# Convolution, GELU and two matmuls: four more blocks in Strassen's form, with more of its sums made by DMA and ScalarE

## The chip, the cores and the metric

The kernel runs on one core of a Trainium2 chip. A core has five engines that run their own instruction lists and wait for each other through semaphores: TensorE (matmul, PE in the profile; PEld is its weight load), VectorE (DVE), ScalarE (ACT), GpSimd (POOL) and SyncE (SP). Sixteen DMA engines move data; transfers are issued from SP, ACT or POOL. On-chip memory is SBUF, and matmuls write to PSUM. The metric is the device time of one launch in microseconds (us).

## The reference

An input `x` of 8 x 4096 tokens with 192 channels is convolved along the tokens, causally, with 7 taps. The taps are a softmax over a weight of 8 heads x 7, and 24 neighbouring channels share a head. The 32768 tokens then go through two matmuls with an exact GELU between them.

```python
w = softmax(weight)                            # 8 heads x 7 taps
x_pad = zeros(B, 6, D) ++ x                    # along the tokens
conv = einsum('hk,bskhg->bshg', w, unfold(x_pad))
h = conv.reshape(32768, 192) @ w_in            # 192 x 2048
g = 0.5 * h * (1.0 + erf(h * inv_sqrt2))
out = g @ w_out                                # 2048 x 192
```

## The kernel before

The tokens are split in two halves of 16384, which lie on partitions 0 to 63 and 64 to 127 and are worked side by side. Each half is cut into 35 blocks (`NB`, L37): six of 256 tokens, then 29 of 512. The 192 channels lie as three groups of 64.

For one block the work goes like this. SP loads `x` as float32 into `xin` (three buffers, `load`, L539; it waits until VectorE has transposed the block three before). VectorE transposes it 32 x 32 into `xT` (`trans`, L706). GpSimd copies six columns of the block before in front of it (`halo`, L639). The seven taps are a multiplication and six multiply-adds on VectorE, each in two pieces of 1024 and 512 columns (`conv`, L731); the last writes `xc` in bf16. For the blocks in `K0` (L73), ScalarE makes the first tap, in three pieces (`first_tap`, L867), at the GELU slots given by `TAPS` of the block two before. TensorE multiplies `xc` by `w_in` (`mm1`, L962) in 16 slices into two PSUM buffers `hp`, and ScalarE turns each slice into bf16 by one GELU into `gT` (L904).

While TensorE makes block n's first product it also makes the second product of block n-1 (`mm2_t`, L1054), interleaved slice by slice. A tile of 64 x 64 of the array is used per matmul, so four matmuls of 512 columns run at once; call four such a round. An ordinary block takes 48 rounds for the first product and 48 for the second. The output, transposed, collects in PSUM banks of `ob`, VectorE transposes it into `osb` (`evac_t`, L363, three per block), and SP stores it (`store`, L551).

Some blocks (`ST`, L72) make the second product in Strassen's form (`mm2_s`, L1101): seven products P1 to P7 in place of eight for two of the three channel groups, plus the ordinary D and E products for the third. That is 44 rounds. It needs sums of halves of `gT` beforehand and sums of the products behind:

- Beforehand: S1 and S3 in four quarters each, Dn and S4 in two halves each (`PART`, L445), written to `sst`. VectorE makes S1, Dn, S4 and the last quarter of S3 (`st_add`, L460). The first three quarters of S3 are two transfers each on GpSimd's queue, a copy and an accumulating one (`st_dma`, L448). Dn needs S1 and S4 needs Dn. The products use them in the order in `TILES` (L378): P5 takes S1, P7 takes S3, P3 takes S4 and P6 takes Dn.
- Behind: six copies on ScalarE (`st_copy`, L484) of P1, P5 and P6 out of PSUM and within SBUF, at slots `AT_COPY`; five sums on VectorE (`st_post`, L503); and three transpositions into `osb` (`st_evac`, L528). TensorE may begin P4 only when the first of these sums (p0) has read its bank, and the next block's second product only when the third (p2) has and P6 is copied.

Every engine works through its list in order. VectorE's order comes from two lists that are merged: `plan` (L764), the taps and input transpositions block by block, and `side` (L796), which says before which step of which block's taps each of the other calls stands (`AT_ST`, `at_ev`). GpSimd's list goes block by block: a halo, then the six transfers of a Strassen block. SP's list goes block by block: the load of three blocks ahead, then a store, which waits for the transpositions.

Of the kernel before, what the change touches and what calls it, by code (L numbers as in the profile page):

```python
# [11 lines left out]
def bass_lightweight_conv__then__act_gelu_exact_kernel(  # L12
# [59 lines left out]
    ST = [m for m in range(M0 + 3, M1) if m % 3 == 0]  # L72
    K0 = {n: i for i, n in enumerate([4, 5, 6, *(n for n in range(9, NB) if n - 3 not in ST)])}  # L73
# [48 lines left out]
    with es:  # L122
# [66 lines left out]
        S_CP = [sem("S_CP%d" % q) for q in range(3)]  # L189
        S_AD = [sem("S_AD%d" % q) for q in range(3)]  # L190
# [116 lines left out]
        def wait_banks(t, m, g):  # L307

            k = G0[m] + g
            if m < M0:  # L310
                if k >= 2:
                    t.wait_ge(S_EVA, k - 1)
            elif g % 2:
                t.wait_ge(S_GELU, SL0[NB] - 1 + g // 2)
            elif M1 - 1 in ST:
                i = ST.index(M1 - 1)
                t.wait_ge(*((S_AC, 6 * i + 4) if g == 0 else (S_EV, EVC[M1] - 2)))
                t.wait_ge(S_DP, 5 * i + 3 + g)
            else:
                t.wait_ge(S_EV, EVC[M1] - 2 + g)  # L320
# [125 lines left out]
        ND = 3  # L446

        def st_dma(e, m, q, h):  # L448

            i, n = ST.index(m), NF // 2 // PART["S3"]  # L450
            dst = ap(sst[1], q * n * TB, [[NF // 2 * TB, 128], [TB, n], [1, TB]])
            src = ap(gT[m % 2], (4 * q * n + h) * TB, [[NF * 2 * TB, 128], [4 * TB, n], [1, TB]])
            if h == 0:
                e.wait_ge(S_GELU, SL0[m] + 2 * (q + 1) * n - 1)
                e.dma_start(dst, src).then_inc(S_CP[q], 16)  # L455
            else:
                e.wait_ge(S_CP[q], 16 * (i + 1))
                e.dma_start(dst, src, accum_op=ALU.add).then_inc(S_AD[q], 16)  # L458

        def st_add(v, m, name, q):  # L460

            g, n = gT[m % 2], NF // 2 // PART[name]

            def a(h, par):
                return ap(g, (2 * q * n + par) * 2 * TB + h * TB, [[NF * 2 * TB, 128], [4 * TB, n], [1, TB]])

            def t(k):
                return ap(sst[k], q * n * TB, [[NF // 2 * TB, 128], [TB, n], [1, TB]])

            i = ST.index(m)  # L470
            v.wait_ge(S_GELU, SL0[m] + 2 * (q + 1) * n)
            if name == "S1":
                ins = v.tensor_tensor(t(0), a(1, 0), a(1, 1), ALU.add)  # L473
            elif name == "S3":
                ins = v.tensor_tensor(t(1), a(0, 0), a(1, 0), ALU.add)
            elif name == "Dn":
                v.wait_ge(S_SA[0], PART["S1"] * i + (q + 1) * n * PART["S1"] // (NF // 2))
                ins = v.tensor_tensor(t(2), a(0, 0), t(0), ALU.add)
            else:
                v.wait_ge(S_SA[2], PART["Dn"] * i + q + 1)  # L480
                ins = v.tensor_tensor(t(3), a(0, 1), t(2), ALU.add)
            ins.then_inc(S_SA[NS.index(name)])

        def st_copy(a, m, k):  # L484

            def xb(r, w=TB):
                return bank(BK[m]["X"], r, w)

            if k > 3:
                a.wait_ge(S_AC, 6 * ST.index(m) + 4)  # L490
            if k in (0, 1, 3):
                st_done(a, m, ("P1", "P5", "", "P6")[k])
            dst, src = (
                (gsm[LO, :], xb(LO)),
                (p5s[UP, :], xb(UP)),
                (p5s[LO, 0 : TB // 2], xb(UP, TB // 2)),
                (uu[LO, :], xb(LO)),
                (uu[UP, :], uu[LO, :]),
                (gsm[UP, :], uu[LO, :]),
            )[k]  # L500
            a.activation(out=dst, in_=src, func=AF.Copy, scale=-1.0 if k > 3 else 1.0).then_inc(S_AC)

        def st_post(v, m, k):  # L503
# [3 lines left out]
            if k == 0:  # L507
                st_done(v, m, "P7")
                v.wait_ge(S_AC, 6 * i + 2)
                ins = v.tensor_tensor(tq[UP, :], bank(BK[m]["Y"], UP), p5s[UP, :], ALU.subtract)  # L510
            elif k == 1:
                st_done(v, m, "P3L")
                v.wait_ge(S_AC, 6 * i + 3)
# [4 lines left out]
            elif k == 3:  # L518
                v.wait_ge(S_AC, 6 * i + 5)
                v.wait_ge(S_DP, 5 * i + 3)  # L520
                ins = v.tensor_tensor(tq[:, :], tq[:, :], uu[:, :], ALU.add)
            else:
                v.wait_ge(S_MM2, MMC[m + 1])
                v.wait_ge(S_AC, 6 * i + 6)
# [3 lines left out]
        def st_evac(v, m, j):  # L528
            i = ST.index(m)
            if j == 2:  # L530
                st_done(v, m, "DE")
                v.wait_ge(S_OUT[m % 2], OUTS[m - 2])
                src = bank(BK[m]["D"])
            else:
                v.wait_ge(S_DP, 5 * i + 5 - j)
                src = (gsm, tq)[j][:, :]
# [14 lines left out]
        def store(e, m):  # L551
# [28 lines left out]
        TAPS = (7, 10, 12)  # L580
        AT_ST = {
            "S1": [(1, 9, 0), (2, 0, 0), (2, 1, 0), (2, 5, -1)],
            "S3": [(2, 5, 1)],
            "Dn": [(2, 0, 2), (2, 5, 2)],
            "S4": [(2, 0, 4), (2, 6, 0)],
            "post": [(2, 11, 0), (3, 0, 0), (3, 2, 0), (3, 6, 0), (3, 9, 0)],
            "ev": [(3, 10, 0), (3, 7, 0), (3, 4, 0)],
        }

        def at_ev(n):  # L590

            if n - 1 in ST:
                return [(2, 15, 0), (3, 4, 0), (3, 4, 0)]
            return [(2, 13, 0) if n == M0 else (3, 0, 3), (3, 5, 0), (3, 5, 0)]

        AT_COPY = {0: (1, 6), 1: (1, 8), 2: (1, 10), 3: (1, 13), 4: (2, 1), 5: (2, 4)}

        @block.gpsimd
        def _(g):
# [72 lines left out]
            for n in range(3, M1 + 2):  # L672
                if n < NB:
                    halo(n)
                if n - 2 in ST:
                    for q, h in ((0, 0), (1, 0), (0, 1), (2, 0), (1, 1), (2, 1)):
                        st_dma(g, n - 2, q, h)

        @block.vector
        def _(v):  # L680
# [83 lines left out]
            plan = []  # L764
            for n in range(2, NB):
                ops = [] if n in K0 else [("t", n, 0)]
                ops += [("c", n, k, q) for k in range(int(n in K0), KS) for q in range(2)]
                if n + 1 in K0:
                    ops[6 if n < 6 else 2 : 6 if n < 6 else 2] = [("t", n + 1, 0)]
                plan.append(ops)  # L770

            def run(op):
                if op[0] == "t":
                    trans(*op[1:])
                else:
                    conv(*op[1:])

# [18 lines left out]
            side = [((M0 + 2, 4 * g, 0), evac, v, M0 - 1, g) for g in range(NG[M0 - 1])]  # L796
            side += [((M0 + 1, 2 * k + 1, 0), weights, v, k) for k in range(6)]
            for n in range(M0, M1):
                todo = []
                if n not in ST:  # L800
                    todo = [(at, evac_t, n, j) for j, at in enumerate(at_ev(n))]
                else:
                    for name, ats in AT_ST.items():
                        for q, at in enumerate(ats):
                            if name == "post":
                                todo.append((at, st_post, n, q))
                            elif name == "ev":
                                todo.append((at, st_evac, n, q))
                            else:
                                todo.append((at, st_add, n, name, q if name != "S3" else ND))  # L810
                side += [((n + at[0], *at[1:]), op, v, *rest) for at, op, *rest in todo]
            for n in range(M1, NB):
                for g in range(NG[n]):
                    side.append(((n + 3, g, 0), evac_half, v, g, 0))
            side.sort(key=lambda q: q[0])
            for b in range(2, NB):
                for o, op in enumerate(plan[b - 2]):
                    while side and side[0][0][:2] <= (b, o):
                        side[0][1](*side[0][2:])
                        side.pop(0)  # L820
                    run(op)
            for q in side:
                q[1](*q[2:])

        @block.scalar
        def _(a):
# [35 lines left out]
            for n in K0:  # L862
                at = taps.get(n, TAPS)
# [54 lines left out]
        def _(t):  # L918
# [135 lines left out]
            def mm2_t(m, ps, i):  # L1054

                w = WS[m]
                if i == 0:
                    if m - 1 in ST:
                        s = ST.index(m - 1)
                        if ps == 0:  # L1060
                            t.wait_ge(S_AC, 6 * s + 4)
                            t.wait_ge(S_DP, 5 * s + 3)
# [38 lines left out]
            def mm2_s(m, e):  # L1101
# [9 lines left out]
                if u == "P6":  # L1111
                    need(S_AC, 6 * i + 1)
                if u == "P4":
                    need(S_DP, 5 * i + 1)
# [5 lines left out]
                else:  # L1120
                    q = NS.index(src)
                    part = k * PART[src] // (NF // 2)
                    if src == "S3" and part < ND:
                        need(S_AD[part], 16 * (i + 1))
                    elif src == "S3":
                        need(S_SA[q], i + 1)
                    else:
                        need(S_SA[q], PART[src] * i + part + 1)
# [80 lines left out]
        def _(sp):  # L1209
# [6 lines left out]
            load(sp, 3)  # L1216
            for n in range(1, NB):
                if n + 3 < NB:
                    load(sp, n + 3)
# [33 lines left out]
```

## Time and profile before

| | |
|---|---|
| median of three runs | 671.5 us (671.0 to 671.69) |
| the profiled execution | 670.93 us |
| its span, first to last instruction | 669.2 us |
| TensorE busy, granted clock | 665.8 us (99%), 1.000 |
| VectorE busy | 604.7 us (90%) |
| ScalarE busy | 587.8 us (88%) |
| GpSimd busy | 91.9 us (14%) |
| packets of hardware / software DMA queues | 49.37 MB, 33.0% / 16.13 MB, 12.1% of the 16 engines' span |
| transfers into `sst` on POOL's queue | 54 of 256 KB |

The busy time is the time in which an engine had at least one instruction at work. The rows of neighbouring instructions on VectorE and ScalarE overlap a little, so the time from start to start is what counts. TensorE's matmul ends are modelled: one row of 376 ns does not mean that a round takes that long. What limits the kernel is read from the chain of work that ended last and from who waits for whom.

### The profile page before, as it was taken

How to read it: one execution, taken by the hardware profiler on the slowest of the kernel's cores; microseconds unless marked ns; L12 is line 12 of the kernel's file. 1: busy time of each engine (PE TensorE's matmuls, PEld its weight loads, DVE VectorE, ACT ScalarE, POOL GpSimd, SP SyncE). 2: the span in 40 equal slices, each digit the busy share in tenths (PEclk: the TensorE clock that was granted, in tenths of full speed). 3: DMA queues.
4: the chain of work that ended last, by engine and by line, in shares of the span. 5: the costliest groups of instructions: out<-in, count | busy, mean ns of one | idle time of the engine just before them, and what ended most of it. 6: DMA issues, size and time to landing. Idle time of an engine off the chain costs nothing.

```text
span 669.2 us, 27224 instructions
## 1 busy us (share of the span) xinstructions
PE 665.8 (99%) x12504; PEld 416.2 (62%) x12504; DVE 604.7 (90%) x703; ACT 587.8 (88%) x659; POOL 91.9 (14%) x115
## 2 busy tenths in 40 slices
PE   9999999999999999999999999999999999999998
PEld 8999655556555655655565556556555655565567
DVE  5989999899999999999999999999999999999633
ACT  8999988899988988898999889888989998898783
POOL 8020000030012003001300120030013001200300
PEclk9999999999999999999999999999999999999999
DMA  9535234273466047515634660485157346602423
GB/s 153 123 86 132 61 72 97 73 132 85 96 143 139 9 96 176 112 36 126 140 84 97 140 143 7 96 176 111 39 127 140 82 97 142 139 8 61 119 63 96
DMA packets 142786, 67.82 MB, mean 101 GB/s; under 512 B 127248, under 2 KB 140880, under 8 KB 142672
## 3 DMA queue, kind: packets, MB, share of 16 engines
q1 hardware_dynamic: 129136, 49.37, 33.0%
q0 software_dynamic: 12416, 16.13, 12.1%
q8 instruction: 98, 1.61, 1.0%
q10 hardware_dynamic: 1120, 0.59, 0.3%
q14 instruction: 16, 0.13, 0.1%
HBM read 28.31 MB, written 25.17 MB: 80 GB/s over the span
## 4 chain that ended last, share of the span: by engine, by line
PE 99%; ACT 0%; DVE 0%; DMA 0%; issue 0%; ACTq 0%
PE hp L999 49%; PE ob L1077 29%; PE ob L1143 13%; PE ob L1039 5%; PE ob L1199 1%; PE hp L1199 1%; PE ob L941 0%; DMA wsb<-in_weight_dram 0%; PE ob L999 0%; ACT dg L846 0%; DVE wcol L701 0%; ACT xc L237 0%; DVE wnm L692 0%; ACT osb L344 0%; ACT wex L833 0%
## 5 line engine op out<-in xcount | busy, mean ns | idle before, releaser
L904 ACT ACTIVATE gT<-hp 128x1024 bf16<-128x1024 f32 x510 | 518.2, 1023 | 68.3 <-PE hp L999 60.5
L999 PE MATMUL hp<-xc,win 64*64 64x512 bf16 (+2 forms) x6036 | 416.8, 366 | 0.1
L757 DVE SCALAR_TENSOR_TENSOR acc<-xT,wcol,acc 128x1024 f32<-128x1024 f32 (+1 forms) x330 | 299.6, 957 | 7.3 <-ACT acc L872 7.3
L999 PEld LDWEIGHTS hp<-xc,win 64*64 64x64 bf16 (+1 forms) x6036 | 190.6, 106 | 126.5 <-ACT xc L237 0.3
L1077 PE MATMUL ob<-gT,wout 64*64 64x512 bf16 x3648 | 248.6, 376 | 0.0
L1077 PEld LDWEIGHTS ob<-gT,wout 64*64 64x64 bf16 x3648 | 116.9, 118 | 83.3
L1143 PE MATMUL ob<-gT,wout 64*64 64x512 bf16 x864 | 109.3, 376 | 0.0
L1143 PE MATMUL ob<-sst,wst 64*64 64x512 bf16 x432 | 88.9, 376 | 0.0
L729 DVE STREAM_TRANSPOSE xT<-xin 128x1536 f32<-128x1536 f32 (+2 forms) x39 | 74.6, 1922 | 9.7 <-DMA xin<-in_x_dram 9.3
L652 POOL COPY xT<-xT 128x18 f32<-128x18 f32 x30 | 28.9, 964 | 330.9 <-DVE xc L757 171.3
L1143 PEld LDWEIGHTS ob<-gT,wout 64*64 64x64 bf16 x864 | 48.8, 118 | 25.2
L757 DVE SCALAR_TENSOR_TENSOR xc<-xT,wcol,acc 128x1024 bf16<-128x1024 f32 (+1 forms) x66 | 61.9, 960 | 0.3
L370 DVE STREAM_TRANSPOSE osb<-ob 128x512 f32<-128x512 f32 x57 | 47.6, 874 | 4.0 <-PE ob L1077 3.7
L455 POOL DMA_DIRECT2D sst<-gT x27 | 19.8, 733 | 175.1 <-ACT gT L904 175.1
L872 ACT ACTIVATE acc<-xT,wcol 128x512 f32<-128x512 f32 (+1 forms) x63 | 43.6, 693 | 0.0
L1039 PE MATMUL ob<-wout,gT 64*128 64x192 bf16 x768 | 41.0, 243 | 0.0
L1143 PEld LDWEIGHTS ob<-sst,wst 64*64 64x64 bf16 x432 | 36.2, 107 | 6.0
L1143 PE MATMUL ob<-gT,wst 64*64 64x512 bf16 x144 | 39.7, 376 | 0.0
L1039 PEld LDWEIGHTS ob<-wout,gT 64*128 64x128 bf16 x768 | 33.4, 94 | 4.8
L458 POOL DMA_DIRECT2D sst<-gT x27 | 33.1, 1227 | 8.0 <-DMA sst<-gT 7.9
L473 DVE TENSOR_TENSOR sst<-gT 128x1024 bf16<-128x1024 bf16 x36 | 24.9, 691 | 10.0 <-ACT gT L904 9.9
L1143 PE MATMUL ob<-sst,wout 64*64 64x256 bf16 x288 | 30.8, 269 | 0.0
(75 smaller groups left out, 268.2 us busy)
## 6 DMA issues: line engine op xcount, KB each, us to landing
out_dram<-osb SPq DMA_DIRECT2D x124, 192.0 KB, 3.4
xin<-in_x_dram SPq DMA_DIRECT2D x116, 192.0 KB, 4.2
sst<-gT POOLq DMA_DIRECT2D x54, 256.0 KB, 4.1
xin<-in_x_dram SPq DMA_DIRECT2D x18, 96.0 KB, 2.4
wout<-in_moe_w_out_dram POOLq DMA_DIRECT2D x4, 192.0 KB, 4.5
win<-in_moe_w_in_dram POOLq DMA_DIRECT2D x4, 96.0 KB, 4.1
win<-in_moe_w_in_dram POOLq DMA_DIRECT2D x2, 192.0 KB, 4.1
xin<-in_x_dram POOLq DMA_DIRECT2D x4, 96.0 KB, 3.9
```

Source lines behind the costliest of these rows:

```text
L370: v.transpose(osb_t(m, j), bank(BK[m][j])).then_inc(S_EV)
L458: e.dma_start(dst, src, accum_op=ALU.add).then_inc(S_AD[q], 16)
L473: ins = v.tensor_tensor(t(0), a(1, 0), a(1, 1), ALU.add)
L652: g.tensor_copy(dst, src).then_inc(S_HALO)
L729: v.transpose(out, src).then_inc(S_TR)
L757: ins = v.scalar_tensor_tensor(dst, src, wk, a, op0=ALU.mult, op1=ALU.add)
L872: a.activation(out=acc[n % 2][:, p * TB : p * TB + w], in_=ap(xT[n % 2], p * XW + HX, [[NP * XW, 128], [1, w]]), func=AF.Copy, scale=wcol[ ...
L904: a.activation(out=ap(gT[n % 2], i * c * 2 * w, dst), in_=ap(ob, 2 * TB, [[4 * TB, 128], *src[1:]]) if u < SL0[1] and u % 3 == 2 else ap(h ...
L999: ins = t.matmul(hbuf(u, slice(fo, fo + fw), o, w), ap(win, f1, [[NP * F, 64], [2, fw]]), xc[n % 2][r, p * TB : p * TB + w], start=(p == 0 ...
L1039: ins = t.matmul(bb[sub], gT[m % 2][r, c0 : c0 + 128], wout[r, CH[sub][i] * C : (CH[sub][i] + 1) * C], start=(ph == 0 and k == 0), stop=(p ...
L1077: ins = t.matmul(bank(BK[m][j], slice(64 * h, 64 * h + 64), w), ap(wout, 64 * hf * NF * C + CH[h][i] * C + j, [[NF * C, 64], [NP, 64]],), ...
L1143: ins = t.matmul(bank(BK[m][bk], slice(64 * cg, 64 * cg + 64), w), wt_, a[r, c0 : c0 + w], start=(e == mine[0]), stop=(e in (mine[-1], GRO ...
```

## The change

- `ST` becomes every second block from 8 to 32: 13 blocks, before 9 (9, 12, ... 33).
- `K0` now has all blocks from 9 on, so ScalarE makes the first tap for all of them. `TAPS` depends on whether the block three before is a Strassen block: slots 5, 8, 11 if not, 10, 12, 15 if so.
- S1's first two quarters become transfers too (`BY_DMA`); `DMAS` gives the order of a Strassen block's ten transfers, and halos and moves are sorted in between.
- Three more transfers, `st_move`: the lower half of `p5s` and the upper half of `gsm`, which ScalarE copied, and the accumulation of `uu` onto `tq`, which VectorE added. `st_copy` is left with four copies, `st_post` with four sums. In the new numbering p0 to p2 are as before and p3 is gsm's sum. The first copy also waits until the Strassen block before has been transposed.
- VectorE's calls come from one string, `ORDER`, with a letter for each call (t input transposition, c tap, w weight sum, 1 3 d 4 the sums S1 S3 Dn S4, p small sum, e output transposition).
- From block 7 on, SP issues a load one block earlier, ahead of the store before it.

```diff
-    ST = [m for m in range(M0 + 3, M1) if m % 3 == 0]
-    K0 = {n: i for i, n in enumerate([4, 5, 6, *(n for n in range(9, NB) if n - 3 not in ST)])}
+    ST = list(range(M0 + 2, M1, 2))
+    K0 = {n: i for i, n in enumerate([4, 5, 6, *range(9, NB)])}
...
+        BY_DMA = [("S3", 0), ("S1", 0), ("S3", 1), ("S1", 1), ("S3", 2)]
+        DMAS = [(3, "S3", 0, 0), (4, "S1", 0, 0), (7, "S3", 1, 0), (8, "S1", 1, 0), (8.1, "S1", 0, 1), (8.2, "S3", 0, 1),
+                (9, "S1", 1, 1), (11, "S3", 2, 0), (11.1, "S3", 1, 1), (12, "S3", 2, 1)]
...
+        def st_dma(e, m, name, q, h):
+
+            out, one, two, done = add_of(m, name, q)
+            if h == 0:
+                e.wait_ge(S_GELU, done)
+                e.dma_start(out, one).then_inc(S_CP[name, q], 16)
+            else:
+                e.wait_ge(S_CP[name, q], 16 * (ST.index(m) + 1))
+                e.dma_start(out, two, accum_op=ALU.add).then_inc(S_AD[name, q], 16)
+
+        def st_move(e, m, k):
+
             i = ST.index(m)
+            e.wait_ge(S_AC, 4 * i + (2, 4, 4)[k])
+            if k == 0:
+                e.dma_start(p5s[LO, 0 : TB // 2], p5s[UP, 0 : TB // 2]).then_inc(S_PS, 16)
+            elif k == 1:
+                e.dma_start(gsm[UP, :], uu[UP, :]).then_inc(S_GU, 16)
+            else:
+                e.wait_ge(S_DP, 4 * i + 3)
+                e.dma_start(tq[:, :], uu[:, :], accum_op=ALU.add).then_inc(S_TQ, 16)
...
-            if k > 3:
-                a.wait_ge(S_AC, 6 * ST.index(m) + 4)
-            if k in (0, 1, 3):
-                st_done(a, m, ("P1", "P5", "", "P6")[k])
+            if k == 0 and m != ST[0]:
+                a.wait_ge(S_EV, EVC[ST[ST.index(m) - 1] + 1])
+            if k < 3:
+                st_done(a, m, ("P1", "P5", "P6")[k])
+            else:
+                a.wait_ge(S_AC, 4 * ST.index(m) + 3)
...
-            elif k == 3:
-                v.wait_ge(S_AC, 6 * i + 5)
-                v.wait_ge(S_DP, 5 * i + 3)
-                ins = v.tensor_tensor(tq[:, :], tq[:, :], uu[:, :], ALU.add)
...
-        TAPS = (7, 10, 12)
-        AT_ST = {
-            "S1": [(1, 9, 0), (2, 0, 0), (2, 1, 0), (2, 5, -1)],
...
-        AT_COPY = {0: (1, 6), 1: (1, 8), 2: (1, 10), 3: (1, 13), 4: (2, 1), 5: (2, 4)}
+        TAPS = ((5, 8, 11), (10, 12, 15))
+        ORDER = (
+            "tccccccccccccccctccctccccccccccccwtccccccccccccwwwwwctcccccccccccccccccccccccttccccccccccccccetceccc"
...
+        )
+        AT_COPY = {0: (1, 6), 1: (1, 8), 2: (1, 13), 3: (2, 1)}
...
-            for n in range(3, M1 + 2):
-                if n < NB:
-                    halo(n)
-                if n - 2 in ST:
-                    for q, h in ((0, 0), (1, 0), (0, 1), (2, 0), (1, 1), (2, 1)):
-                        st_dma(g, n - 2, q, h)
+            work = [((n - 2, 0), halo, n) for n in range(3, NB)]
+            for m in ST:
+                for at, name, q, h in DMAS:
+                    work.append(((m, at), st_dma, g, m, name, q, h))
+                work += [((m + 1, 8.5), st_move, g, m, 0), ((m + 2, 2), st_move, g, m, 1), ((m + 2, 3), st_move, g, m, 2)]
+            for _, op, *rest in sorted(work, key=lambda q: q[0]):
+                op(*rest)
...
+            nxt = 4
             for n in range(1, NB):
-                if n + 3 < NB:
-                    load(sp, n + 3)
+                while nxt < min(NB, n + (4 if n < M0 + 1 else 5)):
+                    load(sp, nxt)
+                    nxt += 1
                 store(sp, n - 1)
```

In `ORDER` two blocks of the steady part are these 43 letters, from an input transposition of an odd block to the next: `t1cccde1ed344cccccpcccptpceccccccccpccecece`. The letter e after d and 1 transposes what an ordinary block left; the three after the last p's transpose the Strassen block.

## The prediction

> **What bounds the kernel now.** First the page: its span and busy shares, and the chain that ended last.
>
> ```profile
> span 669.2 us, 27224 instructions
> ...
> PE 665.8 (99%) x12504; PEld 416.2 (62%) x12504; DVE 604.7 (90%) x703; ACT 587.8 (88%) x659; POOL 91.9 (14%) x115
> ...
> PE 99%; ACT 0%; DVE 0%; DMA 0%; issue 0%; ACTq 0%
> ```
>
> TensorE is the whole chain, at a granted clock of 1.0; nobody else sets the end. Second, the busy time in three following blocks, cut where ScalarE starts each block's first GELU (18 is a Strassen block, so its second product lies in the first line).
>
> ```profile
> 330.43:350.29 19.86, 19.86 (x389) 12.27 (x384) 18.97 (x21) 17.90 (x20) 0.71 (x1) 1.00 0.35 82
> 350.29:371.01 20.72, 20.72 (x389) 11.77 (x384) 19.15 (x22) 19.04 (x21) 1.19 (x1) 1.00 0.37 78
> 371.01:391.73 20.72, 20.72 (x389) 11.77 (x384) 20.46 (x24) 17.89 (x19) 6.58 (x7) 1.00 0.71 154
> ```
>
> Columns: window, length, then busy PE, PE weight load, DVE, ACT, POOL. A block costs TensorE 20.72 us, or 19.86 where it holds a Strassen product: 92 rounds of four matmuls in place of 96, at 0.216 a round. Per three blocks VectorE works 58.6 of 61.3 us, ScalarE 54.8. Third, VectorE's own steps, from its timeline in the third window; the difference of two starts is the price, since a row's duration overlaps the next by some 0.1.
>
> ```profile
> 372.06 1.60 DVE L370 STREAM_TRANSPOSE osb<-ob 128x512 f32<-128x512 f32 x2
> ...
> 377.87 0.68 DVE L473 TENSOR_TENSOR sst<-gT 128x1024 bf16<-128x1024 bf16 x1
> 378.47 1.93 DVE L757 SCALAR_TENSOR_TENSOR acc<-xT,wcol,acc 128x1024 f32<-128x1024 f32 x2
> 380.33 1.93 DVE L757 SCALAR_TENSOR_TENSOR xc<-xT,wcol,acc 128x1024 bf16<-128x1024 f32 x2
> 382.19 0.68 DVE L473 TENSOR_TENSOR sst<-gT 128x1024 bf16<-128x1024 bf16 x1
> 382.97 1.23 DVE L478 TENSOR_TENSOR sst<-gT,sst 128x2048 bf16<-128x2048 bf16 x1
> 384.11 0.90 DVE L370 STREAM_TRANSPOSE osb<-ob 128x512 f32<-128x512 f32 x1
> 384.88 1.18 DVE L481 TENSOR_TENSOR sst<-gT,sst 128x2048 bf16<-128x2048 bf16 x1
> ```
>
> A tap (1024 and 512 columns) steps 1.86, S1 0.60, Dn 1.14, S4 1.10, an output transposition 0.77. Fourth, the transfers that take the place of VectorE sums: the copy's row, then the accumulating one's.
>
> ```profile
> DMA to landing us min/median/max: 2.4/3.7/5.8
> ```
> ```profile
> DMA to landing us min/median/max: 3.6/4.1/6.5
> ```
>
> **The change, part by part.** Nine Strassen blocks become thirteen. Each saves TensorE 20.72 - 19.865 = 0.855, so 4 x 0.855 = 3.42 us. That is all on the path, if no new wait appears. The profiled execution took 670.93 (span 669.2, 1.7 around it); 670.93 - 3.42 = 667.5. The median of the three shown is 671.5, 0.57 above it: 668.1.
>
> *VectorE.* Per two blocks it now has 12 taps of 1.86 (22.3; the ScalarE first tap is everywhere, which drops L750's 0.75 + 0.46), two input transpositions of 2.25 (4.5), six output ones (4.6), two S1 (1.2), one S3 (0.56), two Dn (2.28), two S4 (2.2), four small sums (0.73, 0.34, 0.46, 0.60 by their steps: 2.1): 39.8 of 20.72 + 19.87 = 40.59 us. Its room falls from 2.7 us in 61 to 0.8 in 41. It stays off the path only if waits take no more than 0.8 per pair.
>
> *Where the list stands against TensorE.* Mark 0 is TensorE's first matmul of an even block, 20.72 the next odd block, which holds the Strassen product, 40.59 the end. The D bank is complete at 0, so its transposition cannot start sooner; adding steps from there: both p3 and the tq transposition at 8.3 and 10.8, gsm's at 12.2 to 13.0, et0 of the odd block at 14.2, the input transposition to 17.2, third S1 17.8, Dn0 20.3 to 21.4, et1 22.2, fourth S1 22.8, et2 23.6, Dn1 24.7, S3 25.3, S4 27.5, p0 32.4 to 33.1, p1 36.0, input transposition 38.2, p2 38.7, a tap 39.9, then 0.8 of waiting for the next D. TensorE's needs I count in rounds of its order: P5 takes the fourth S1 in the third slice, behind 9 rounds of first product and 6 of second, 15 x 0.216 = 3.2 into the odd block; P4 follows 33 and 28 rounds, 13.2. So: et0 20.7, fourth S1 24.0, S3 27.6, S4 28.7, p0 33.9, p2 41.2. p0's own inputs are there by 31.7 (in the block after 18 the like p5s copy ended 10.95 into the block). Every one holds; the tightest is p0, by 0.8. Before, p0 of block 18 ended 341.69, 11.9 into the odd block, against 13.2: 1.3 of room.
>
> *Transfers on POOL's queue.* Per Strassen block ten, before six; S1's first two quarters are new. Each issue takes POOL 0.73 (copy) and up to 1.2 (adding); 13 issues with the three moves, some 12 of 40.6 us, and the halo copies queued behind them are wanted 10 us later. The late one is S1's second quarter: 8 GELUs are done at 11.0, the copy issues there and lands 2.4 to 5.8 later, its adding transfer 3.6 to 6.5 after that: 17.0 to 23.3. VectorE's Dn0 wants it at 20.3, TensorE's P5 at 21.8. I take 19.3: the copy near its short end, since SP is quiet then; the adding one near 5.7, since gsm's transposition at 13.0 releases four stores and four loads of 192 KB at just that time. S3's third quarter: 11 GELUs at 15.1, copy inside that burst (5), adding 5: 25.2 against 26.5; bounds 21.1 to 27.4.
>
> *ScalarE.* p5s's lower half, gsm's upper half and VectorE's tq sum become transfers: two copies less per Strassen block (0.41 and 0.66 a step). But the odd block gets the first taps (0.61 a step) at slots 10, 12, 15 beside copies at 6, 8, 13; before, block 13 had copies alone. 16 GELUs at 1.02 plus 3 x 0.61 plus 0.48, 0.62, 0.48, less 0.1 overlap at six places, 19.2 of 19.87. Laid against arrivals of hp (1.08, 1.295, 1.51 apart), the second GELU of the next block ends 0.1 before TensorE wants its buffer. Cost taken 0, at most some 0.1 per pair, 1.3 us. The moves: p5s's transfer leaves at 31.7 and has till 35.6 (p1); gsm's and tq's leave at 2.7 to 4.7, have till 8.3 and 10.8; 6.5 at worst by the row above. At nothing, covered by taps. If p5s's came 1 us late, p2 has 2.5 to spare.
>
> *SP.* Loads go one block earlier: this removes a wait of 1.2 in "DVE xT L729 <- DMA xin" per three blocks. Off the path: 0. *Start.* The weight sums move into VectorE's idle 1.8 + 0.8 before blocks 5 and 6; block 7's taps end at 82.2 in place of 82.4: 0. *Tail.* No Strassen block ends it any more; the last groups' 2.6 us of matmuls are the same: 0, perhaps -0.4.
>
> A rule that speaks against it: the Trainium skill, "DMA: Bandwidth & Descriptors", section "SWDGE vs HWDGE vs iDMA", says GpSimd writes the descriptors of its transfers into SBUF state that VectorE can lock it out of. POOL's 27 copy issues took 716 to 746 ns although VectorE worked 90% of the span, so no row shows it; by the rule each issue ahead of S1's second quarter could lose one VectorE step of 1.2 (an estimate), five of them 6 us, and the total would be the first rival's. The same page, "Queues, rings and completion order": engines go round robin between queues, packet by packet, by which the adding transfer would land near its 3.6 and nothing would wait; the rows' 6.5 beside SP's traffic speak against counting on it.
>
> **Rivals.** *S1's second quarter lands late (slower).* From 21.05 on, Dn0's start pushes p0 past P4's 33.9 (it follows by 12.85), from 21.8 P5 waits too. At 23.3 P5 loses 1.5 and P4 0.75 more: 2.25 x 13 = 29 us, 697. At 22.3: 0.5 + 0.75, 16 us, 684. It turns slower above 0.37 per pair, a landing at 21.4. For it: the burst at 13.0 and a DMA share of 0.71 in the window with six transfers; against: half the adding transfers landed within 4.1.
>
> *VectorE becomes the bound (slower).* Were its idle 2.7 per three blocks kept, 1.8 per two, a pair would take 41.6: 1.0 x 12.5 = 13 us, 680. Against: those waits (ACT p5s 7.2 in 9, DMA xin 9.3 in 8) show VectorE early, and go when it is later.
>
> *ScalarE or small lateness eats the gain (no change).* 0.26 per pair is 3.4 us: 671.
>
> **How the numbers follow.** No wait on TensorE: 0.60, 667.3 to 670. Late transfer 0.19, VectorE 0.10, gain eaten 0.11. A difference of 0.2% (1.3 us) is about what measurement tells from none. Faster 0.60; same 0.10; slower 0.30 (both slow rivals and a bit of the third). Low 667.2 is the sum with the tail's 0.4 and hardly any of the 0.57 between profile and median; high 682 takes in VectorE's case and the milder half of the late transfer, leaving some 0.13 above.
>
> **What would show it.** Right: odd blocks with an even one before at 19.87 throughout, pairs of 40.59, VectorE waiting about 0.8 per pair for "PE ob", PE still 99%. Wrong: PE idle before L1143 matmuls out of sst, released by a DMA (late S1 or S3) or by DVE tq (p0); VectorE without idle time and pairs over 40.6; PE idle before hp, released by ACT.

## The result and the profile after

The changed kernel takes 751.02 us (748.67 to 752.74, four runs) against 671.26 (671.0 to 671.69, four runs): 1.1185 times the time before, 95% interval 1.1153 to 1.1217. The forecast was 668.1, range 667.2 to 682.0. The profiled execution took 750.51, its span 748.7.

The page of the changed kernel, the same lines as before:

```profile
span 748.7 us, 27413 instructions
...
PE 689.8 (92%) x12504; PEld 473.6 (63%) x12504; DVE 613.9 (82%) x704; ACT 596.2 (80%) x681; POOL 177.4 (24%) x230
...
PE 57%; DMA 18%; issue 10%; POOL 8%; DVE 4%; ACT 2%; DVEq 0%; POOLq 0%; ACTq 0%
```

TensorE is no longer the whole chain. A quarter of it is transfers (DMA) and the engine that issues the sums' transfers (POOL). Of the part called issue, 76 us, 62 us are POOL's as well: stretches of up to 8 us between one addition's issue and the next one's. VectorE and ScalarE do about the work that they did, in a longer span. Next two pairs of blocks, cut again at the first GELU of 20, 21, 22, 23 and 24 (columns: window, length, busy PE, PE weight load, DVE, ACT, POOL, granted clock, DMA share, GB/s):

```profile
388.72:409.24 20.52, 20.52 (x385) 13.36 (x381) 19.18 (x22) 18.40 (x21) 10.03 (x11) 1.00 0.62 139
409.24:434.66 25.42, 20.87 (x393) 14.39 (x388) 20.69 (x23) 18.82 (x23) 2.53 (x4) 1.00 0.68 137
434.66:455.18 20.52, 20.52 (x387) 13.72 (x381) 19.22 (x22) 18.40 (x22) 10.00 (x11) 1.00 0.63 141
455.18:481.61 26.43, 22.56 (x393) 15.02 (x388) 20.71 (x23) 18.96 (x23) 2.16 (x4) 0.94 0.63 130
```

The even blocks lose nothing; the whole loss lies in the odd ones, which hold the Strassen products. (An even block reads 20.52 and an odd one 20.06 where nothing waits, since the first GELU after a Strassen product now starts 0.2 later; the pair is 40.59.) In the last line the granted clock is 0.94. The 13 odd blocks take 23 to 29 us in place of 19.87. Their excess is 84 us, less 2.4 from the even blocks that are 0.2 shorter. Who waited for whom, the lines that concern TensorE and the sums:

```profile
POOL sst L497 <- DMA sst<-gT: 82.4, 17, 8.2
...
PEld ob L1129 <- DMA sst<-gT: 63.3, 33, 3.8
PE ob L1129 <- DMA sst<-gT: 48.1, 29, 3.3
DVE sst L487 <- DMA sst<-gT: 38.1, 13, 3.6
```

L1129 is the matmul of `mm2_s`, L497 the adding transfer of `st_dma`. TensorE's idle stretches from block 8 on, taken one by one by the semaphore that ended each, are 54.1 us in all: 31.7 stood before S3's third quarter, 13.5 before S1's second, 3.0 before S3's second, 4.2 before a sum of VectorE (which had itself waited for S1) and 1.7 before p0. So the transfers are late. The adding transfers' row reads:

```profile
DMA to landing us min/median/max: 3.6/7.2/12.4
```

Before, its median was 4.1 and its longest 6.5. The longest copy went from 5.8 to 10.3. POOL's list then waits: the last adding transfer may not be issued until its copy has landed. In block 20, the first of the blocks shown above, this is 6.85 us of waiting at 412.35 in the timeline of POOL:

```profile
399.13 0.71 POOL L494 DMA_DIRECT2D sst<-gT  x1 [0.59 <-ACT gT L896]
399.82 3.71 POOL L497 DMA_DIRECT2D sst<-gT  x3
403.23 1.05 POOL L494 DMA_DIRECT2D sst<-gT  x1
403.96 1.54 POOL L497 DMA_DIRECT2D sst<-gT  x1
412.35 1.18 POOL L497 DMA_DIRECT2D sst<-gT  x1 [6.85 <-DMA sst<-gT]
```

In just this stretch SP issued its four stores, from 400.76, and its four loads, from 405.01 to 410.85.

### The profile page after: what moved, and what is told of

It reads as the page before. It is cut to its first block, busy times and chain, and to the rows that moved or that the text cites. A ratio compares the mean times of both kernels' runs of the same rounds, so it can differ in the third digit from the quotient of the medians.

```text
span 748.7 us, 27413 instructions
## 1 busy us (share of the span) xinstructions
PE 689.8 (92%) x12504; PEld 473.6 (63%) x12504; DVE 613.9 (82%) x704; ACT 596.2 (80%) x681; POOL 177.4 (24%) x230
## 4 chain that ended last, share of the span: by engine, by line
PE 57%; DMA 18%; issue 10%; POOL 8%; DVE 4%; ACT 2%; DVEq 0%; POOLq 0%; ACTq 0%
PE hp L991 29%; DMA sst<-gT 17%; PE ob L1129 12%; PE ob L1069 11%; POOL sst L497 6%; PE ob L1031 4%; ACT gT L896 2%; POOL sst L494 2%; DVE sst L487 1%; DVE acc L775 1%; PE ob L1185 1%; PE hp L1185 1%; DMA xin<-in_x_dram 1%; DVE xc L775 1%; DVE xT L747 0%
## 5 line engine op out<-in xcount | busy, mean ns | idle before, releaser
L991 PE MATMUL hp<-xc,win 64*64 64x512 bf16 (+2 forms) x6036 | 479.5, 374 | 1.1 <-DVE xc L775 1.0
L991 PEld LDWEIGHTS hp<-xc,win 64*64 64x64 bf16 (+1 forms) x6036 | 237.3, 107 | 105.2 <-issue 8.9
L1129 PE MATMUL ob<-gT,wout 64*64 64x512 bf16 x1248 | 207.8, 392 | 0.0
L1069 PE MATMUL ob<-gT,wout 64*64 64x512 bf16 x2880 | 205.6, 376 | 0.0
L1129 PE MATMUL ob<-sst,wst 64*64 64x512 bf16 x624 | 143.3, 402 | 52.5 <-DMA sst<-gT 48.1
L1069 PEld LDWEIGHTS ob<-gT,wout 64*64 64x64 bf16 x2880 | 112.2, 118 | 47.7
L1129 PEld LDWEIGHTS ob<-sst,wst 64*64 64x64 bf16 x624 | 53.3, 112 | 84.5 <-DMA sst<-gT 63.3
L1129 PEld LDWEIGHTS ob<-gT,wout 64*64 64x64 bf16 x1248 | 93.6, 121 | 19.6 <-issue 2.5
L497 POOL DMA_DIRECT2D sst<-gT x65 | 84.3, 1424 | 90.1 <-DMA sst<-gT 82.4
L487 DVE TENSOR_TENSOR sst<-gT,sst 128x2048 bf16<-128x2048 bf16 x52 | 61.7, 1207 | 38.1 <-DMA sst<-gT 38.1
L494 POOL DMA_DIRECT2D sst<-gT x65 | 52.0, 800 | 72.5 <-ACT gT L896 72.2
L1129 PE MATMUL ob<-gT,wst 64*64 64x512 bf16 x208 | 57.4, 376 | 1.7 <-DVE tq L534 1.7
L1129 PE MATMUL ob<-sst,wout 64*64 64x256 bf16 x416 | 48.8, 275 | 0.0
L1129 PEld LDWEIGHTS ob<-sst,wout 64*64 64x64 bf16 x416 | 39.5, 122 | 3.3
```

The source lines that it names most:

```text
L487: v.tensor_tensor(out, one, two, ALU.add).then_inc(S_SA[NS.index(name)])
L494: e.dma_start(out, one).then_inc(S_CP[name, q], 16)
L497: e.dma_start(out, two, accum_op=ALU.add).then_inc(S_AD[name, q], 16)
L991: ins = t.matmul(hbuf(u, slice(fo, fo + fw), o, w), ap(win, f1, [[NP * F, 64], [2, fw]]), xc[n % 2][r, p * TB : p * TB + w], start=(p == 0 ...
L1069: ins = t.matmul(bank(BK[m][j], slice(64 * h, 64 * h + 64), w), ap(wout, 64 * hf * NF * C + CH[h][i] * C + j, [[NF * C, 64], [NP, 64]],), ...
L1129: ins = t.matmul(bank(BK[m][bk], slice(64 * cg, 64 * cg + 64), w), wt_, a[r, c0 : c0 + w], start=(e == mine[0]), stop=(e in (mine[-1], GRO ...
```

## The experiments

Three theories stood at the start. A: the sums' transfers land late because SP's burst of eight transfers runs beside them. B: ten transfers per Strassen block are too slow on GpSimd's queue by themselves. C: VectorE's list is too long, and the transfers only show it. All times below have the kernel before beside them at 671.0 to 671.2. Where no number of runs is given, the time is that of one run; where a kernel ran eleven times, its times spread over 2.9 us. Landing times are medians over the 13 Strassen blocks. They are in us from 0.65 before the even block's first GELU, which is where the prediction's own figures have their mark 0. By the prediction's count TensorE wants S1's second quarter at 21.8 and S3's third at 26.5.

### S1 back on VectorE

```diff
-        BY_DMA = [("S3", 0), ("S1", 0), ("S3", 1), ("S1", 1), ("S3", 2)]
+        BY_DMA = [("S3", 0), ("S3", 1), ("S3", 2)]
...
-            "...t1cccde1ed344..."
+            "...t111cccde1ed344..."
```

> All four quarters of S1 are VectorE sums again (36 of the 130 sum transfers... 52 of them go, 78 stay); everything else as in the changed kernel. Theory A (the sums' transfers land late because SP's burst of eight transfers runs beside them) and theory B (ten sum transfers per Strassen block are too slow on GpSimd's queue by themselves) both say: no wait for S1, S3's third quarter two transfers sooner; VectorE has 39.8 + 2 x 0.60 = 41.0 us of work per pair against 40.59, so about 673 us, 668 to 690. Theory C (VectorE's list is what is too long, the transfers are symptoms): not below 751.

Measured: 682.4 us, within what A and B expect; C as the cause of 751 falls. But VectorE now has more work than a pair has time. One pair in that kernel:

```profile
395.00:436.25 41.25, 40.50 (x765) 30.08 (x760) 41.06 (x46) 36.63 (x43) 8.95 (x11) 1.00 0.59 128
```

VectorE works 41.06 of 41.25 us where 41.0 was the sum, and paces the pair. S3's third quarter, now behind six transfers per block and still beside SP's burst, lands at 26.6 in place of 31.4, and is late at times (5 us of TensorE's idle time).

### SP holds the Strassen block's store

```diff
                     nxt += 1
+                if n - 1 in ST and n + 1 in ST:
+                    sp.wait_ge(S_AD["S3", 2], 16 * (ST.index(n + 1) + 1))
                 store(sp, n - 1)
```

> SP holds the store of a Strassen block until the next Strassen block's last S3 transfer has landed, so that its burst of four stores and four loads no longer runs beside the sums' transfers. Theory A: S1's second quarter lands about 19 us into the even block in place of 23.3, S3's third quarter before 26.5, the waits of 31.7 and 13.5 us vanish, 668 to 680 us. Theory B: odd blocks stay over 24 us, time over 725.

Measured: 673.7 us. All ten transfers are there, and the adding one's row is back to

```profile
DMA to landing us min/median/max: 3.6/4.2/9.4
```

S1's second quarter lands at 18.4 (22.7 in the changed kernel), S3's third at 23.8 (31.4). The odd blocks are between 19.87 and 20.66, most of them 20.06, but for the first, 24.12. This decides for A against B: ten transfers are no hindrance if SP is quiet. In the first Strassen block SP's burst was that of block 6's store, which this edit does not hold.

### The loads elsewhere, the stores alone, and copies for additions

Three runs take away parts of the collision. In the first, SP issues two loads at every odd step and none at even ones, so that only four stores meet the sums there:

```diff
-                while nxt < min(NB, n + (4 if n < M0 + 1 else 5)):
+                while nxt < min(NB, n + (4 if n < M0 + 1 else 5 + int(n > 8 and n % 2))):
```

> At every odd step from 9 on SP issues two loads, at even ones none, so the burst beside the sums' transfers is four stores and no load. Theory A: about half of the loss goes, 700 to 725 us. Theory B: 740 to 755.

In the second, the loads alone are held:

```diff
+                if n in ST:
+                    sp.wait_ge(S_AD["S3", 2], 16 * (ST.index(n) + 1))
                 while nxt < min(NB, n + (4 if n < M0 + 1 else 5)):
```

> Only the four loads are held until the last S3 transfer has landed; the Strassen block's four stores go out beside the sums' transfers as in the changed kernel. Theory A with delay in proportion to SP's bytes in the way: S1's second quarter near 20.5 into the even block (22.7 with both, 18.4 with neither), S3's third near 27 (31.4, 23.8), 680 to 705 us. If the stores alone did the harm: over 730; if the loads alone: under 676.

In the third, SP's burst stays and the second transfer of each sum is a copy; this kernel leaves the addition out and serves for its time alone:

```diff
-                e.dma_start(out, two, accum_op=ALU.add).then_inc(S_AD[name, q], 16)
+                e.dma_start(out, two).then_inc(S_AD[name, q], 16)
```

> The second transfer of each sum copies in place of adding, which leaves the sum out; the number of transfers, bytes and waits stay. In the trace a copy ran as 64 packets of 4 KB at 0.16 us, an adding one as 256 packets of 1 KB at 0.10 us, 2.5 times the time of the engines. Theory B: the queue has room again, waits for sums vanish, 668 to 685 us. Theory A: SP's burst still delays them, waits fall by a third at most, over 715 us.

| what runs beside the sums | time | S1's second | S3's third |
|---|---|---|---|
| four stores, four loads (the change) | 751.0 | 22.7 | 31.4 |
| four stores; loads two ahead | 717.2 | 22.3 | 28.6 |
| four stores; loads held | 701.7 | 22.4 | 27.6 |
| four stores, four loads; copies for additions | 696.1 | 19.4 | 27.6 |
| nothing (store and loads held) | 673.7 | 18.4 | 23.8 |

The first two came out in A's bounds. The stores alone make S1 nearly as late as the whole burst does (A expected 20.5); S3 gets 3.8 of its delay from the stores and 3.8 more from the loads that follow them. The third fell between the theories: copies helped more than A said and less than B said. An addition runs as 256 packets of 1 KB at 0.10 us and a copy as 64 of 4 KB at 0.16, so A has to be put more exactly: what delays a sum is SP's burst together with the sums' own packets queued ahead of it. Putting copies for the additions gave back 55 us, holding the loads 49, holding all of SP 77.

The packets of the traces say the same. From 14 to 24 us into the even block the sums' packets alone fill 0.85 of the 16 engines' time where SP is quiet (median of the 13 blocks); in the changed kernel SP's packets take 0.39, and 0.66 is left to GpSimd's queue. So the engines are full there, though their share over a whole pair is 0.65.

### Both holds

The 673.7 left two things: the first Strassen block, and odd blocks a few tenths over 20.06. First block 6's store is held as well:

```diff
-                if n - 1 in ST and n + 1 in ST:
+                if n + 1 in ST:
```

> As the run in which SP holds a Strassen block's store, and block 6's store too, so that the first Strassen block (8) also has its sums' transfers alone. There that block's odd neighbour still took 24.1 us in place of 20.06, with one wait of 2.1 for S1. Theory A: this goes too, 673.7 - 4.1 = 669.6, between 668.5 and 671; the first version below the kernel before. Theory B: no change, 673 to 674.5.

Measured: 671.24 us (670.36 to 673.22, eleven runs), 0.9998 of the kernel before, interval 0.9989 to 1.0008. The first odd block is 20.06 as expected, but in the trace (of an execution of 672.56) blocks 10, 16 to 19, 23 and 33 are 0.2 to 0.9 too long, and the median missed 669.6 and just missed the range up to 671. The waits show what is late now:

```profile
DVE tq L538 <- DMA p5s<-p5s: 10.4, 6, 2.6
...
PEld ob L1129 <- DVE tq L534: 2.5, 5, 0.7
```

The p5s transfer, moved from ScalarE by the change, now meets SP's burst that was put off: it lands 4.8 us after its issue (median). So the ordinary block's store, and with it the loads behind, is held in its turn. The lines that are added to the edit before:

```diff
+                if n in ST:
+                    sp.wait_ge(S_PS, 16 * (ST.index(n) + 1))
                 store(sp, n - 1)
```

> As the run before, and SP also holds the ordinary block's store until the p5s transfer has landed. Under the single hold that transfer took 4.6 us beside SP's burst (1.9 alone), VectorE waited 6.4 us for it in all, and four odd blocks were 0.2 to 0.6 over 20.06, behind p0. Theory A (any transfer beside SP's burst is late, and the list has no room for it): these go, 667.5 to 669. Rival: p0 is late for VectorE's own sum of 39.8 of 40.59, whatever the transfers; the same as the single hold within 0.5 us.

Measured: 668.5 us (667.82 to 669.11, five runs), 0.9953 of the kernel before, interval 0.9939 to 0.9967, and faster than both kernels. Its page, and one pair:

```profile
span 666.5 us, 27439 instructions
...
PE 662.3 (99%) x12504; PEld 474.6 (71%) x12504; DVE 611.2 (92%) x704; ACT 594.9 (89%) x681; POOL 189.3 (28%) x230
...
PE 98%; DMA 1%; POOL 0%; issue 0%; DVE 0%; ACT 0%; POOLq 0%
```
```profile
410.00:450.59 40.59, 40.59 (x776) 29.63 (x772) 39.77 (x44) 37.23 (x43) 11.32 (x15) 1.00 0.69 156
```
```profile
DVE tq L538 <- DMA p5s<-p5s: 2.3, 4, 0.9
```

The p5s transfer now lands in 2.8 us (median), and the trace shows no idle stretch of TensorE between block 6 and the end. The rival, that p0 is late for VectorE's own sum, falls: VectorE's work is the same, and the time went down 2.7. The DMA share of the pair, 0.69, is higher than the 0.65 of the changed kernel's pair above: the transfers are the same, and what changed is which of them meet.

## Why the prediction was wrong

- *TensorE's saving, 3.42 us, and the sum 668.1.* Near, where no transfer is late: the pair is 40.59 to the hundredth, and the kernel with both holds takes 668.5. Against the 671.2 beside it that saves 2.7 of the 3.42; in its trace block 6 starts 0.5 later than before, and block 19 is 0.2 too long.
- *VectorE's 39.8 per pair.* Right: 39.77. Its room of 0.8 was enough there, but less than one late p5s transfer cost with the single hold (up to 2.6).
- *The list's marks.* Right: SP's burst was put at 13.0 and its first store issues at 12.7. Where no transfer is late, in block 20 of the kernel with both holds, p0 ends at 32.8, for 33.1.
- *Transfers on POOL's queue: "I take 19.3" and "25.2".* This is the step that failed: the burst was foreseen, and the time that a transfer takes beside it was put too low. S1's second quarter landed at 22.7, within the bounds given; S3's third at 31.4, outside 21.1 to 27.4. The upper bound of 6.5 for an adding transfer was no bound: the rows of before held three additions per Strassen block with at most the end of a burst beside them, and here several queue one behind the other with eight transfers of SP among them. The medians by transfer are 8.2 (S1's second addition, taken as 5.7), 8.6 (S3's third copy, taken as 5) and 7.0 (S3's third addition, taken as 5). S3's two are in series, so its error is the sum of both. The trace of before could have told it: its eight additions with packets of SP beside them took 5.0 to 6.5, the nineteen without 3.6 to 4.7 (one 5.6). Half of them "within 4.1" was thus no evidence for a transfer inside the burst.
- *The first rival.* Its mechanism was the right one, with a chance of 0.19 and at most 29 us. The loss in the blocks was 82 us. It looked at S1 only, and S3's third quarter cost 31.7 of the 54.1 us of idle time. It also left out the clock: 34.1 us in odd blocks at half the granted clock cost about 34.1 x 0.5 = 17 more (an estimate). Some 11 us are not split further here; the idle stretches are measured from matmul ends that are modelled, so each may be a little too short.
- *SP's loads one block earlier, "off the path: 0".* Loads are not off the path where they ride in the burst behind the store: holding them alone gave back 49 us. That the block earlier is to blame is not shown: in SP's list, and in the trace of before, loads follow right behind a store as well, and no run takes this part back.
- *The moves.* "If p5s's came 1 us late, p2 has 2.5 to spare" was true of p2, but not of VectorE's whole list, which the wait pushes into the next pair: 671.24 against 668.5.
- *ScalarE and the second rival.* ScalarE's margin of 0.1 held: no idle stretch of TensorE from block 6 on in the last kernel. VectorE became the bound only where S1 was put back on it, 41.06 for an expected 41.0.
- *The rules of the skill.* Of the page "DMA: Bandwidth & Descriptors", the lock on descriptor writing shows little: the copies' issues took 708 to 1467 ns, median 716 (732 before), mean 800 (733 before). The round robin between queues did not protect the sums as the prediction read it, with an addition landing near 3.6: the changed kernel's median is 7.2. The page's rule says who is served next, not that the engines have room.

## What to carry to other kernels

A transfer's latency in a profile holds for what ran beside it then; for a change that adds transfers, set each issue time against every other queue's bursts, and price the queue in front of it, not the row's maximum. A chain of transfers in series (copy, wait, add) adds such errors up, and where an engine has 0.8 us of room in 40.6, a wait of 2.6 comes through. The cure was two waits on SP, which has time: hold bulk loads and stores until the transfers that others wait for have landed.

## What the runs showed of the hardware

TensorE's granted clock fell to a half after idle stretches. In the changed kernel, stretches of 2.67 to 3.33 us before S3's third quarter were followed by 3.4 us (once 6.8) at 0.5, in nine odd blocks of 13; one of 2.61 us was not:

```profile
226.30:229.90 3.60, 3.60 (x42) 2.12 (x38) 2.67 (x3) 1.89 (x3) 0.00 (x0) 0.53 1.15 232
```

Length alone did not decide: with copies for additions a stretch of 2.04 us was followed by it, with the loads two ahead one of 2.75 us was not. What decided can be worked out from the traces. The times at which the clock fell lie whole multiples of 3.413 us apart within each run (226.38, 274.17 and 321.95: 14 such steps from each to the next). Cut blocks 6 to 33 into windows of 3.413 us on that grid, over seven traces: each of the 15 full-speed windows with 2.04 us or more of TensorE's idle time was followed by one at half speed, and none of those with 2.00 or less was. The 2.75 us fell into two windows, 1.34 and 1.41. (The 6.8 us are two windows: the first, at half speed, held 0.99 us of idle time itself.) The Trainium skill, "TensorE: Matmul & The Clock Gate", section "Part 1: The HAM clock gate (the "warmup" mystery)", tells of such a fall to half speed after an idle window of about 3.4 us that runs free of the kernel; here 2.04 of the 3.41 were enough. So a wait of 2 to 3 us can cost TensorE another 1.7 us (3.4 at half speed).

Beside SP's burst GpSimd's queue moved unevenly. In the trace's packets of the changed kernel, between 404 and 405 us, SP's queue moved 583 packets and GpSimd's 4, with additions waiting; between 405 and 406 it was 106 and 119. From 402 to 412 us the packets of the two queues filled 0.39 and 0.66 of the 16 engines' time, 1.05 in all. Why single microseconds went almost wholly to SP no run here shows.
